# Splitting the end of a transformer block's backward pass into two streams with their own buffers

## The chip, the cores and the metric

The kernel runs on one core of one Trainium2 chip. The metric is the device time of one execution in microseconds, as the median of several runs. One further execution is taken with the hardware profiler; its page and its trace are what the text reads.

## The reference, cut to what matters

The program computes a decode step of a block (attention with a KV cache, then a ReLU MLP, each behind a layernorm) and all its gradients except for those of two constants. B = 2 sequences, D = 640, H = 32 heads of Dh = 128, Sk = 4096 cached positions, Dff = 1728, all in bfloat16.

```python
q = (x @ wq).reshape(B, Sq, Hq, Dh).transpose(0, 2, 1, 3)
scores = jnp.einsum("bhqd,bhkd->bhqk", q, k) * (Dh ** -0.5)
p = softmax(scores, axis=-1)
o = jnp.einsum("bhqk,bhkd->bhqd", p, v)
attn = o.transpose(0, 2, 1, 3).reshape(B, Sq, Hq * Dh) @ wo
...
h = x + A(layernorm(x), k_cache, v_cache, wq, wo)
h2 = h + relu(layernorm(h) @ w1) @ w2
_out, _vjp = jax.vjp(_f, A_x, A_k_cache, A_v_cache, A_wq, A_wo, B_w1, B_w2)
```

Outputs: out_0 is h2, out_1 the gradient of x, out_2 and out_3 those of the K and V caches (64 tiles of 1 MB each), out_4 that of wq (640 x 4096), out_5 of wo (4096 x 640), out_6 of w1 (640 x 1728), out_7 of w2 (1728 x 640). With one query position per sequence every gradient of a cache tile is an outer product of two vectors, and every gradient of a weight is a sum of two outer products, one for each sequence.

## The kernel before, in words

A *head* here is one of the 64 pairs of a sequence and a head. The work has two passes over the heads.

The first pass (`p1_iter`, 66 iterations, to about 500 us) loads K and V of each head, transposes K on TensorE, makes scores, softmax and the head's output. Between its steps run pieces of the small chains (`middle_gen`): the attention output, the MLP, the backward pass through it, and, head group by head group, the gradient that reaches each head's output (`go_group`). A chain may run ahead only as far as its results exist; the marks ("w1", b), ("gh1", b) and ("go", b, h) in `done` say how far it is.

The second pass (`p2_iter`, from iteration 44 of the first pass on beside it, from about 500 us on alone) loads V again for 53 of the heads (tile `Wt`; 11 are kept from the first pass). For a head j it transposes V in four groups of four fp32 transposes (L374), copies each from PSUM on ScalarE (`t_sb`, L379), multiplies them with the output's gradient (L387), and makes the two gradient tiles on VectorE: gV of head j from the softmax (L789, L791, the multiply is L735), and gK of head j - 1 (L769, L772), after `gsp` (L748), which needs the products of all four groups. Each half tile is one VectorE instruction. The stores of gK (L773) and gV (L792) are issued on GpSimd's queue (POOL); loads are issued on SyncE's (SP).

*Buffers.* 12 buffers of 8 KB per partition, each tagged by a home, serve everything of 1 MB: "ld" for loads and "g" for gradient tiles (3, then 4, then 5 of them). `take` hands out the one that came free first; `give` returns it in program order, so that whoever takes it next waits on the engine for its last use, also for a store that is still under way. The weight gradients' tiles `ot`, the pieces of wq that are read again (`wqs`) and the pieces of w2 read again (`w_t` in `mlp_out`) come out of "ld" as well, as long as one or two are free (`spare`, `reserve`).

*The end of the work.* When ("w1", 1) is done and the first pass is over, w1's memory is released and one background generator, `fin_gen`, is started in the queue `bg2`. In order it makes: rows of the MLP's activations (`rows_of`: a copy to `wide`, four matmuls with the identity, a copy back), out_7, rows, out_6, rows, out_5, in `outer_rows`. After each stored piece of out_6 and out_5 it may read one of six pieces of wq again (`gx_piece`: 30 transposes of wq, then 30 small matmuls into the x gradient), once all heads concerned have passed. Then come the rest of these pieces, the x gradient's layernorm backward, the two row stores of out_1, the rows of GQ and x1, and out_4. `outer_rows` makes three outer products of 512 or 128 columns into three PSUM banks ("mid", "m", "a"), casts them on ScalarE one after the other (L840), and stores a tile of about 1 MB from GpSimd's queue (L842). `store_row` (L572) transposes a row vector and stores it from SyncE's queue, out of one buffer `orow`.

*The order.* All instructions are placed by hand: the loop over `plan` steps `p2_iter`, and after each of its seven steps per head calls `bg_step`, which gives each background queue a credit (here `RATE2` = 0.85 per step); a generator yields what a piece of it costs (0.5 per outer product, 0.9 per eight wq transposes). Every engine executes its own instructions strictly in this order. What is left when the heads are through is run out at once (L1088 to L1091).

Of the kernel before, what the change touches and what calls it, by code (L numbers as in the profile page):

```python
# [15 lines left out]
def kernel(  # L16
# [60 lines left out]
    homes = {"ld": list(range(NBIG)), "g": []}  # L77
    free = {"ld": NBIG, "g": 0}
    owned = {"ld": NBIG, "g": 0}
    stores = [0]  # L80
    spare = [2]
    home_of = {}

    def take(tag, shape, name):
        assert free[tag] > 0, (tag, name)
        free[tag] -= 1
        k = homes[tag].pop(0)
        t = big.tile(shape, BF16, tag=f"big{k}", bufs=1, name=name)
        home_of[id(t)] = (tag, k, t)
        return t  # L90

    def give(t, to=None):
        tag, k, _ = home_of.pop(id(t))
        to = to or tag
        owned[tag] -= 1
        owned[to] += 1
        free[to] += 1
        homes[to].append(k)

    def share(n):  # L100

        stores[0] = n
        while owned["g"] < n and free["ld"] > 0:
            homes["g"].append(homes["ld"].pop(0))
            for d in (free, owned):
                d["ld"] -= 1
                d["g"] += 1
# [464 lines left out]
    def store_row(col_bf, n, dst):  # L572

        t = pst([16, 128], BF16, "mid", "row_ps")
        nc.tensor.transpose(t[0:n, :], col_bf, ident_bf[:])
        r = small.tile([16, 128], BF16, tag="orow", bufs=1, name="orow")
        nc.vector.tensor_copy(out=r[0:n, :], in_=t[0:n, :])
        nc.sync.dma_start(out=dst, in_=r[0:n, :])
# [47 lines left out]
    def mlp_out():  # L626

        ml32 = small.tile([128, ND, B], FP32, tag="ml32", bufs=1, name="ml32")
        nc.vector.memset(ml32[:], 0.0)
        for k in range(NW2):  # L630
            while free["ld"] < spare[0]:
                yield
            t = load_w2(k, "ld")
            yield from wait(8)
            c1 = min(NF, (k + 1) * FP)
            m_ps = pst([128, ND, B], FP32, "mid", "mlp_ps")
            for c in range(ND):
                for cf in range(k * FP, c1):
                    kc = f_kc(cf)
                    nc.tensor.matmul(m_ps[:, c, :], lhsT=t[0:kc, cf - k * FP, c * 128:(c + 1) * 128],  # L640
                                     rhs=acol[0:kc, cf, :], start=(cf == k * FP), stop=(cf == c1 - 1))
            give(t)
            yield
            nc.vector.tensor_tensor(out=ml32[:], in0=m_ps[:], in1=ml32[:], op=ALU.add)
        ml_bf = small.tile([128, ND, B], BF16, tag="ml_bf", bufs=1, name="ml_bf")
        nc.vector.tensor_copy(out=ml_bf[:], in_=ml32[:])
        y_bf = small.tile([128, B, ND], BF16, tag="y_bf", bufs=1, name="y_bf")
        nc.vector.tensor_tensor(out=y_bf[:].rearrange("p b c -> p c b"), in0=h1c[:], in1=ml_bf[:], op=ALU.add)
        yield from wait(3)
        for b in range(B):  # L650
            store_row(y_bf[:, b, :], ND, out_0[b].rearrange("s (c p) -> (s c) p", p=128))
            yield
# [87 lines left out]
    def p2_iter(j, busy):  # L740
# [45 lines left out]
        give(c["W"], "g" if owned["g"] < stores[0] else "ld")  # L786
# [31 lines left out]
    def outer_rows(L, nrow, R, N, out_ap, cc, between=None):  # L818


        P = nrow // cc
        grp = max(1, min(cc, 4096 // N))
        out_v = out_ap.rearrange("(p c) n -> p c n", c=cc)
        for c0 in range(0, cc, grp):
            gn = min(grp, cc - c0)
            while free["ld"] < spare[0]:
                yield
            ot = take("ld", [128, grp, N], "ot")
            todo = [(k, n0, min(512, N - n0)) for k in range(gn) for n0 in range(0, N, 512)]
            for t0 in range(0, len(todo), 3):  # L830
                part = []
                for k, n0, nn in todo[t0:t0 + 3]:
                    q = 32 * (fw[0] % 4)
                    o_ps = pst([128, 512], FP32, ("mid", "m", "a")[len(part)], "o_ps")
                    nc.tensor.matmul(o_ps[0:P, 0:nn], lhsT=L[q:q + B, bass.ds(c0 + k, P, step=cc)],
                                     rhs=R[q:q + B, n0:n0 + nn], start=True, stop=True)
                    part.append((o_ps, k, n0, nn))
                    fw[0] += 1
                for o_ps, k, n0, nn in part:
                    nc.scalar.copy(out=ot[0:P, k, n0:n0 + nn], in_=o_ps[0:P, 0:nn])  # L840
                yield 0.5 * len(part)
            nc.gpsimd.dma_start(out=out_v[:, c0:c0 + gn, :], in_=ot[0:P, 0:gn, :])  # L842
            give(ot)
            if between is not None:
                yield from between()

    def fin_gen(fin):
        gx1 = fin.tile([128, ND, B], FP32, tag="gx1", name="gx1")
        nc.vector.memset(gx1[:], 0.0)
# [3 lines left out]
        yield from wait(4)  # L853
        gx_next = [0]

        def gx_piece(k):

            hn = min(QP, H - k * QP)
            while free["ld"] < spare[0]:
                yield  # L860
            t = take("ld", [128, ND, QP * 128], "wqs")
            nc.sync.dma_start(out=t[:, :, 0:hn * 128], in_=wq_r[:, :, k * QP * 128:(k * QP + hn) * 128])
            yield from wait(6)
# [3 lines left out]
            for t0 in range(0, len(todo) + GT, GT):  # L867
                part = todo[t0:t0 + GT]
                nxt = None
                if part:  # L870
                    t_ps = pst([128, GT, 128], BF16, "tps", "t_ps")
                    for x, (c, j) in enumerate(part):
                        nc.tensor.transpose(t_ps[:, x, :], t[:, c, j * 128:(j + 1) * 128], ident_bf[:])
                    t_sb = mats.tile([128, GT, 128], BF16, tag="XT", bufs=5, name="t_sb")
                    nc.scalar.copy(out=t_sb[:, 0:len(part), :], in_=t_ps[:, 0:len(part), :])
                    nxt = (t_sb, part)
                    if t0 + GT >= len(todo):
                        give(t)
                    yield 0.9
                if prev is not None:  # L880
                    if acc is None:
                        acc = pst([128, ND, B], FP32, "m", "gx_ps")
# [4 lines left out]
                    yield  # L887
                prev = nxt
            nc.vector.tensor_tensor(out=gx1[:], in0=gx1[:], in1=acc[:], op=ALU.add)

        def gx_ready():

            k = gx_next[0]
            if k < NQ and all(("go", B - 1, h) in done for h in range(k * QP, min(H, (k + 1) * QP))):
                gx_next[0] += 1
                yield from gx_piece(k)

        yield from rows_of(fin, acol, NF, "ar", "rF")
        yield from rows_of(fin, gc, ND, "gr", "rD")
        yield from outer_rows(FIN["ar"], Dff, FIN["gr"], D, out_7, Dff // 96)  # L900
        yield from rows_of(fin, ghfc, NF, "ghfr", "rF")
        yield from rows_of(fin, x2c, ND, "x2r", "rD")
        yield from outer_rows(FIN["x2r"], D, FIN["ghfr"], Dff, out_6, ND, gx_ready)
        while ("gh1", B - 1) not in done:
            yield
        yield from rows_of(fin, OFc, H, "OFr", "rH")
        yield from rows_of(fin, gh1c, ND, "gh1r", "rD")
        yield from outer_rows(FIN["OFr"], HD, FIN["gh1r"], D, out_5, HD // 128, gx_ready)
        while gx_next[0] < NQ:
            yield from gx_ready()  # L910
            yield
# [4 lines left out]
        for b in range(B):  # L916
            gxo = small.tile([128, ND], BF16, tag="gxo", bufs=2, name="gxo")
            nc.vector.tensor_copy(out=gxo[:], in_=gx_bf[:, :, b])
            store_row(gxo[:], ND, out_1[b].rearrange("s (c p) -> (s c) p", p=128))
            yield  # L920
        yield from rows_of(fin, GQc, H, "GQr", "rH")
        yield from rows_of(fin, x1c, ND, "x1r", "rD")
        yield from outer_rows(FIN["x1r"], D, FIN["GQr"], HD, out_4, ND)
# [3 lines left out]
    bg2 = []  # L927
    done = set()
    credit = [0.0, 0.0]
# [15 lines left out]
    def bg_step(k, rate):  # L945
        step[0] += k
        q = (bg, bg2)[k]
# [17 lines left out]
    RATE2 = 0.85  # L965
# [30 lines left out]
    reserve = [0]  # L996

    def pump():
        while queue:
# [3 lines left out]
            else:  # L1003
                tag = "ld"
                if free["ld"] <= reserve[0]:
# [12 lines left out]
    fin = None  # L1018
# [12 lines left out]
    for n, (i, j) in enumerate(plan):  # L1031
# [3 lines left out]
        if j == 0:  # L1035
            stores[0] = 3
        if i is None and plan[n - 1][0] is not None:
            share(4)
        if j == H + KEPT[1]:
            share(5)  # L1040
# [6 lines left out]
        reserve[0] = 2 if bg2 and j is not None and j >= H + 4 else 0  # L1047
        spare[0] = 1 if j is not None and j >= H + 2 else 2
        if i is None and ("w1", 1) in done and fin is None:
            wts.release()  # L1050
            fin = tc.alloc_tile_pool(name="fin", bufs=1)
            bg2.append(("fin", fin_gen(fin)))
        if i == 12:
# [3 lines left out]
        if i is None:  # L1057
            spread[0] = 2
            k = 0
            while g2 is not None:  # L1060
# [5 lines left out]
                bg_step(1, RATE2)  # L1066
            continue
        at = MIXED if j is not None else REST
        for k, _ in enumerate(p1_iter(i, i < H + 1, int(H + 1 < i < P2_AT))):
# [15 lines left out]
            bg_step(1, RATE2)  # L1085
# [4 lines left out]
    while bg2:  # L1090
        bg_one(bg2)  # L1091
# [32 lines left out]
```

## Time and profile before

| | |
|---|---|
| median of 3 runs | 1010.29 us (1006.11 to 1011.26) |
| profiled execution, its own time | 1006.34 us |
| its span | 1004.6 us |
| PE, PEld, DVE, ACT, POOL busy | 786.2, 693.8, 657.1, 587.3, 108.3 us |
| mean granted clock of PE | 0.794 |
| HBM read, written | 212.16 MB, 149.13 MB |
| first and last ot cast (L840) | 692.0 and 997.1 us |
| wqs loads issued (L862), six | 746.5 to 917.9 us |
| last store of gV, of gK issued | 944.9 us, 952.7 us |

A page of the profile gives, for each engine, the busy time, then the span cut into 40 equal slices, then the DMA queues (q1 is the hardware queue of SyncE's loads, q0 the software queue of GpSimd's stores), the chain of work that ended last, and groups of instructions by source line. A line such as

```profile
L840 ACT CAST ot<-o_ps 128x512 bf16<-128x512 f32 (+4 forms) x160 | 66.3, 492 | 23.9 <-DMA out_dram<-ot 15.1
L842 POOL DMA_DIRECT2D out_dram<-ot x17: 519/531/547, 708.4 to 998.1; - x17
```

reads: line 840 of the kernel, on ScalarE, casts `o_ps` to `ot`, 160 times in five shapes, 66.3 us busy, 492 ns each on average; the engine stood idle 23.9 us just before such an instruction, most of it, 15.1 us, for the store of an `ot` tile. The second line (from the answer for one tile) gives shortest, median and longest duration in ns of the instruction that issues a store, and the first and last start in us. The duration is that of the issue, not of the transfer.

### The profile page before, as it was taken

Reading aid. Unit: us, or ns where it says so; the run is one execution under the profiler, and the core shown is the slowest. Engines: PE = TensorE matmul, PEld = TensorE weight load, DVE = VectorE, ACT = ScalarE, POOL = GpSimd, SP = SyncE. Lnnn points to the kernel's source line nnn. Section 1 sums busy time; section 2 is a strip of 40 time slices with the busy share of each in tenths; the row PEclk is TensorE's granted clock in tenths of the full one; section 3 lists DMA queues with packets and bytes.
Section 4 is the critical chain, followed back from the end, with each engine's and each line's share of the span. In section 5 each row is a group of like instructions: output and inputs, shape, how many; then the busy total and the mean of one; then the engine's idle time right before and its main releaser. Section 6 shows DMA issues by size and latency. Waiting matters only on the chain.

```text
span 1004.6 us, 30245 instructions
## 1 busy us (share of the span) xinstructions
PE 786.2 (78%) x13169; PEld 693.8 (69%) x13173; DVE 657.1 (65%) x1289; ACT 587.3 (58%) x1261; POOL 108.3 (11%) x219
## 2 busy tenths in 40 slices
PE   5999999999899989999968646558485938865846
PEld 5988898999888888888867545446364727654611
DVE  3555776755486687878788897998683726653600
ACT  4666666667677767777644433335363718554747
POOL 0000000000000010000012121212121212211201
PEclk8899999999799999999995756777565658555555
DMA  9999999995587799999999999999799998999735
GB/s 351 417 400 394 350 380 412 380 373 185 197 297 279 276 346 381 422 421 421 389 365 420 424 370 425 420 425 419 298 385 399 403 407 322 421 424 417 314 123 209
DMA packets 63205, 363.25 MB, mean 362 GB/s; under 512 B 5696, under 2 KB 20928, under 8 KB 22880
## 3 DMA queue, kind: packets, MB, share of 16 engines
q1 hardware_dynamic: 42416, 212.18, 54.3%
q0 software_dynamic: 20656, 149.14, 35.8%
q8 instruction: 103, 1.69, 0.7%
q14 instruction: 30, 0.25, 0.1%
HBM read 212.16 MB, written 149.13 MB: 360 GB/s over the span
## 4 chain that ended last, share of the span: by engine, by line
PE 45%; DMA 25%; DVE 10%; issue 10%; ACT 8%; POOL 1%; SPq 0%; POOLq 0%; DVEq 0%; ACTq 0%
PE t_ps L353 10%; PE m_ps L408 10%; DMA wqs<-in_A_wq_dram 8%; PE t_ps L374 7%; DMA out_dram<-gV 6%; DMA Kt<-in_A_k_cache_dram 5%; DMA out_dram<-gK 4%; PE m_ps L423 4%; DVE gV L735 4%; ACT t_sb L358 4%; PE s_ps L364 4%; DVE gK L735 3%; PE dp_ps L387 2%; ACT t_sb L379 1%; PE t_ps L345 1%
## 5 line engine op out<-in xcount | busy, mean ns | idle before, releaser
L358 ACT COPY t_sb<-t_ps 128x1024 bf16<-128x1024 bf16 x223 | 219.6, 1015 | 51.5 <-PE t_ps L353 49.4
L379 ACT COPY t_sb<-t_ps 128x512 f32<-128x512 f32 x256 | 148.9, 589 | 110.9 <-PE t_ps L374 107.9
L408 PE MATMUL m_ps<-pk,Vt 128*128 128x129 bf16 x2048 | 200.3, 225 | 4.3 <-issue 4.3
L374 PE MATMUL t_ps<-ident_f,Wt 128*128 128x128 f32 x848 | 186.5, 368 | 3.8 <-DMA Wt<-in_A_v_cache_dram 2.6
L735 DVE TENSOR_TENSOR gK<-rb,gsp 128x2048 bf16<-128x2048 bf16 x128 | 152.1, 1227 | 32.2 <-DMA out_dram<-gV 18.5
L415 DVE TENSOR_TENSOR pk<-Kt,ep 128x2048 bf16<-128x2048 bf16 x128 | 156.0, 1219 | 24.5 <-ACT ep L465 24.5
L735 DVE TENSOR_TENSOR gV<-rb,pp 128x2048 bf16<-128x2048 bf16 x128 | 152.2, 1218 | 23.1 <-DMA out_dram<-gK 11.1
L353 PE MATMUL t_ps<-ident_bf,Kt 128*128 128x128 bf16 x2048 | 153.0, 224 | 5.8 <-issue 3.8
L374 PEld LDWEIGHTS t_ps<-ident_f,Wt 128*128 128x128 f32 x848 | 133.0, 190 | 17.6 <-issue 9.3
L408 PEld LDWEIGHTS <-Vt 128*128 128x128 bf16 x2048 | 132.5, 101 | 14.3 <-issue 9.1
L353 PEld LDWEIGHTS <-Kt 128*128 128x128 bf16 x2048 | 126.7, 100 | 9.7 <-issue 5.2
L387 PEld LDWEIGHTS <-t_sb 128*128 128x128 bf16 x2048 | 91.5, 105 | 50.3 <-ACT t_sb L379 40.0
L387 PE MATMUL dp_ps<-gom,t_sb 128*128 128x2 bf16 x2048 | 94.3, 167 | 23.5 <-ACT t_sb L379 22.5
L364 PE MATMUL s_ps<-qc,t_sb 128*128 128x1 bf16 x2048 | 89.0, 164 | 13.4 <-ACT t_sb L358 9.5
L364 PEld LDWEIGHTS <-t_sb 128*128 128x128 bf16 x2048 | 79.4, 97 | 18.3 <-ACT t_sb L358 13.4
L840 ACT CAST ot<-o_ps 128x512 bf16<-128x512 f32 (+4 forms) x160 | 66.3, 492 | 23.9 <-DMA out_dram<-ot 15.1
L792 POOL DMA_DIRECT2D out_dram<-gV x64 | 34.2, 534 | 391.5 <-DVE gV L735 279.8
L356 DVE COPY t_sb<-t_ps 128x1024 bf16<-128x1024 bf16 x33 | 22.8, 691 | 68.3 <-PE t_ps L353 68.3
L518 ACT ACTIVATE MT<-m_ps,rtot 128x128 bf16<-128x128 f32 x64 | 23.6, 369 | 69.0 <-PE m_ps L408 64.7
L423 PE MATMUL m_ps<-ep,Kt 128*128 128x1 bf16 x2048 | 60.7, 163 | 1.3 <-ACT OU L519 1.2
L773 POOL DMA_DIRECT2D out_dram<-gK x64 | 34.0, 531 | 255.1 <-DVE gK L735 217.9
L423 PEld LDWEIGHTS <-Kt 128*128 128x128 bf16 x2048 | 58.4, 96 | 1.6 <-issue 1.1
(186 smaller groups left out, 871.2 us busy)
## 6 DMA issues: line engine op xcount, KB each, us to landing
Kt<-in_A_k_cache_dram SPq DMA_DIRECT2D x64, 1024.0 KB, 10.6
Vt<-in_A_v_cache_dram SPq DMA_DIRECT2D x64, 1024.0 KB, 8.6
out_dram<-gV POOLq DMA_DIRECT2D x64, 1024.0 KB, 11.3
out_dram<-gK POOLq DMA_DIRECT2D x64, 1024.0 KB, 11.1
Wt<-in_A_v_cache_dram SPq DMA_DIRECT2D x53, 1024.0 KB, 10.9
wo_t<-in_A_wo_dram SPq DMA_DIRECT2D x4, 1280.0 KB, 11.3
out_dram<-ot POOLq DMA_DIRECT2D x5, 1024.0 KB, 4.1
wq_t<-in_A_wq_dram SPq DMA_DIRECT2D x5, 960.0 KB, 10.3
```

Source lines behind the costliest of these rows:

```text
L353: nc.tensor.transpose(t_ps[:, j, :], nat[:, g * GT + j, :], ident_bf[:])
L358: nc.scalar.copy(out=t_sb[:], in_=t_ps[:])
L364: nc.tensor.matmul(dst[:, sc:sc + 1], lhsT=t_sb[:, j, :], rhs=vec, start=True, stop=True)
L374: nc.tensor.transpose(t_ps[:, j, :], natf[:, 2 * cc:2 * cc + 2, :].rearrange("p c k -> p (c k)"), ident_f[:])
L379: nc.scalar.copy(out=t_sb[:], in_=t_ps[:])
L387: nc.tensor.matmul(dst[:, sc:sc + 2], lhsT=v[:, j, :, par], rhs=vecs[:, par, :], start=(par == 0), stop=(par == 1))
L408: nc.tensor.matmul(r["m"][:, 0:129], lhsT=r["V"][:, sc, :], rhs=r["pk"][sc // HALF][:, sc % HALF, 0:129], start=False, stop=(sc == NSC - 1))
L415: nc.vector.tensor_tensor(out=p["pk"][k][:, :, 0:128].rearrange("p s (a two) -> p s a two", two=2), in0=p["K"][:, sl, :].rearrange("p s (a ...
L423: nc.tensor.matmul(r["m"][:, 129:130], lhsT=r["K"][:, sc, :], rhs=r["ep"][:, sc, 0:1], start=(sc == 0), stop=False)
L735: nc.vector.tensor_tensor(out=pairs_view(dst[:, sl, :]), in0=row.rearrange("p (a two) -> p a two", two=2)[:, None, :, :].to_broadcast([128 ...
L792: nc.gpsimd.dma_start(out=natural(out_3, b, h), in_=gV[:])
L840: nc.scalar.copy(out=ot[0:P, k, n0:n0 + nn], in_=o_ps[0:P, 0:nn])
```

## The change

The weight gradients and the x gradient become two background generators.

- *Two streams.* `fin_gen` now makes only the weight gradients, in the order out_7, out_6, out_5, out_4, the last two in two halves of 16 heads each. `gx_gen` makes the x gradient through wq, in a third queue `bg3` with a credit of its own (`RATE3` = 0.45 per step; `RATE2` is 0.65), from the time that the gradients of all heads' outputs exist.
- *Buffers.* Two more homes: "f" for `ot` tiles, "q" for pieces of wq and of w2. One more buffer of 8 KB (`big2`, in the memory that w1 leaves) is the first of home "f". `share` now states how many each home is to have; a buffer that is given back goes to the home that lacks one. When 36 heads of the second pass have begun: ld 4, g 4, f 3, q 2; when both streams are through: ld 7, g 6. Until then "f" has its one buffer and "ld" eight.
- *Outer products* go one by one through one PSUM bank, matmul and cast in separate steps; when the gradients of all heads' outputs exist, every third cast is done by VectorE (`late`). The tile is stored from ScalarE's queue.
- The x gradient's sums move from PSUM bank "m" to "a"; the next piece of wq is fetched as soon as a buffer of "q" is free; `orow` has two buffers.

```diff
-    homes = {"ld": list(range(NBIG)), "g": []}
-    free = {"ld": NBIG, "g": 0}
-    owned = {"ld": NBIG, "g": 0}
-    stores = [0]
-    spare = [2]
+    homes = {"ld": list(range(NBIG)), "g": [], "f": [], "q": []}
+    free = {tag: len(v) for tag, v in homes.items()}
+    owned = dict(free)
+    wanted = {}
+    pools = [big] * NBIG
...
+    def goes_to(tag):
+
+        if owned[tag] > wanted.get(tag, NBIG):
+            for other in homes:
+                if owned[other] < wanted.get(other, 0):
+                    return other
+        return tag
...
-        to = to or tag
+        to = to or goes_to(tag)
...
+    def more_home(tag, pool):
+        homes[tag].append(len(pools))
+        pools.append(pool)
+        free[tag] += 1
+        owned[tag] += 1
...
-        r = small.tile([16, 128], BF16, tag="orow", bufs=1, name="orow")
+        r = small.tile([16, 128], BF16, tag="orow", bufs=2, name="orow")
...
-            while free["ld"] < spare[0]:
+            while free["q"] < 1:
                 yield
-            t = load_w2(k, "ld")
+            t = load_w2(k, "q")
...
-            ot = take("ld", [128, grp, N], "ot")
+            ot = take("f", [128, grp, N], "ot")
             todo = [(k, n0, min(512, N - n0)) for k in range(gn) for n0 in range(0, N, 512)]
-            for t0 in range(0, len(todo), 3):
-                part = []
-                for k, n0, nn in todo[t0:t0 + 3]:
-                    q = 32 * (fw[0] % 4)
-                    o_ps = pst([128, 512], FP32, ("mid", "m", "a")[len(part)], "o_ps")
...
-                for o_ps, k, n0, nn in part:
+            for x, (k, n0, nn) in enumerate(todo):
+                q = 32 * (fw[0] % 4)
+                fw[0] += 1
+                o_ps = pst([128, 512], FP32, "m", "o_ps")
+                nc.tensor.matmul(o_ps[0:P, 0:nn], lhsT=L[q:q + B, bass.ds(c0 + k, P, step=cc)],
+                                 rhs=R[q:q + B, n0:n0 + nn], start=True, stop=True)
+                yield 0.3
+                if late[0] and x % 3 == 0 and x < len(todo) - 1:
+                    nc.vector.tensor_copy(out=ot[0:P, k, n0:n0 + nn], in_=o_ps[0:P, 0:nn])
+                else:
                     nc.scalar.copy(out=ot[0:P, k, n0:n0 + nn], in_=o_ps[0:P, 0:nn])
-                yield 0.5 * len(part)
-            nc.gpsimd.dma_start(out=out_v[:, c0:c0 + gn, :], in_=ot[0:P, 0:gn, :])
+                yield 0.3
+            nc.scalar.dma_start(out=out_v[:, c0:c0 + gn, :], in_=ot[0:P, 0:gn, :])
             give(ot)
-            if between is not None:
-                yield from between()
...
+    def gx_gen(fin):
...
+        def fetch():
+            while len(tiles) < NQ and free["q"] > 0:
+                k = len(tiles)
+                hn = min(QP, H - k * QP)
+                t = take("q", [128, ND, QP * 128], "wqs")
+                nc.sync.dma_start(out=t[:, :, 0:hn * 128], in_=wq_r[:, :, k * QP * 128:(k * QP + hn) * 128])
+                tiles.append(t)
+
+        while not all(("go", B - 1, h) in done for h in range(H)):
+            yield 0.0
...
-            share(4)
-        if j == H + KEPT[1]:
-            share(5)
+            share(ld=KEPT[1] + 3, g=4)
+        if fin is not None and not bg2 and not bg3:
+            share(ld=7, g=6)
+        elif fin is not None and j >= H + KEPT[1] - 1:
+            share(ld=4, g=4, f=3, q=2)
...
-        reserve[0] = 2 if bg2 and j is not None and j >= H + 4 else 0
-        spare[0] = 1 if j is not None and j >= H + 2 else 2
...
+            big2 = tc.alloc_tile_pool(name="big2", bufs=1)
+            more_home("f", big2)
             bg2.append(("fin", fin_gen(fin)))
+            bg3.append(("gx", gx_gen(fin)))
+        late[0] = all(("go", B - 1, h) in done for h in range(H))
```

## The prediction

> **What bounds the kernel now.** I read the 40 slices of the page first, then the busy time by stretches from 500 us on (the first pass over the heads ends at about 500 us, and nothing that the diff touches runs before 588 us), then who waited for whom on the engines and on SyncE's queue between 700 and 950 us, and last the timeline of the tail. The columns of the first fence are the stretch, its length, busy us and number of instructions of PE, PEld, DVE, ACT and POOL, the granted clock, the DMA share and GB/s.
>
> ```profile
> 500.00:600.00 100.00, 67.28 (x888) 59.84 (x886) 82.72 (x143) 42.90 (x91) 19.57 (x39) 0.67 0.99 396
> 600.00:700.00 100.00, 64.00 (x779) 54.75 (x777) 86.48 (x145) 43.33 (x88) 19.19 (x39) 0.70 1.01 420
> 700.00:750.00 50.00, 29.25 (x281) 22.08 (x282) 36.43 (x65) 25.75 (x65) 10.12 (x21) 0.57 0.89 343
> 750.00:825.00 75.00, 49.42 (x595) 42.72 (x593) 38.30 (x46) 33.99 (x62) 14.72 (x27) 0.59 1.00 406
> 825.00:840.00 15.00, 10.44 (x144) 9.34 (x144) 8.05 (x11) 8.27 (x15) 2.02 (x4) 0.63 0.64 228
> 840.00:925.00 85.00, 58.07 (x644) 46.83 (x641) 48.60 (x51) 46.31 (x99) 15.35 (x32) 0.62 1.01 422
> 925.00:955.00 30.00, 26.91 (x233) 18.75 (x231) 18.25 (x24) 22.41 (x53) 6.15 (x14) 0.56 0.81 328
> 955.00:1005.00 50.00, 25.09 (x83) 7.67 (x81) 1.70 (x10) 27.78 (x64) 3.60 (x7) 0.50 0.39 162
> ```
>
> From 600 us the DMA engines are the bound wherever they are fed: share 1.01 at 420 to 422 GB/s. There are three places where they aren't: 700 to 750 us, 825 to 840 us, and everything after 925 us, above all the last 50 us at 162 GB/s.
>
> ```profile
> PEld L873 <- DMA wqs<-in_A_wq_dram: 44.8, 4, 16.8
> DVE orow L577 <- DMA out_dram<-orow: 18.6, 1, 18.6
> ACT ot L840 <- DMA out_dram<-ot: 15.1, 1, 15.1
> SPq L395 <- DMA out_dram<-ot: 120.9, 5, 40.0
> 952.72 0.53 POOL L773 DMA_DIRECT2D out_dram<-gK  x1 [7.28 <-DVE lb_prod L233]
> 981.28 0.53 POOL L842 DMA_DIRECT2D out_dram<-ot  x1 [24.44 <-ACT ot L840]
> 998.06 0.53 POOL L842 DMA_DIRECT2D out_dram<-ot  x1 [3.66 <-ACT ot L840]
> ```
>
> The first four lines (waits, 700 to 950 us: total, times, longest) name the holes: PE stood 44.8 us for wq pieces, VectorE once 18.6 us for a row buffer, ScalarE once 15.1 us for a weight store to leave its buffer, and SyncE's queue held the loads of V 120.9 us for such stores. The last three (timeline) are the tail: the last store of the second pass is issued at 952.7 us, then come the x gradient's layernorm, the row copies of GQ and the five stores of out_4, the last at 998.1 us. Nothing of the second pass is left to run beside them.
>
> **What the Trainium skill says.** "DMA: Bandwidth & Descriptors", "Issuing engines are not separate DMA queues": transfers started by the scalar, sync and gpsimd engines share 16 engines, and more issuers save only issue time. The trace agrees: two queues together stop at 422 GB/s. So moving stores to ScalarE's queue brings no bandwidth. Its "Queues, rings and completion order" says that an engine takes the rows in turn, packet by packet; here POOL's queue moves stores while SyncE's loads, but no run here shows a third queue. Its "Anatomy of one DMA — SWDGE (gpsimd) path" says that a wait happens on the issuing sequencer, and prices a transfer at 2.0 us + bytes/436e3: 4.4 us for 1 MB. The trace has 4.1 us as the median of the 1 MB stores in the empty tail. "TensorE: Matmul & The Clock Gate", "Part 1: The HAM clock gate", says that a busy PE gets its full clock back; the trace has 0.70 at 64% busy and 0.50 in the tail, so denser PE work should not run slower.
>
> **The change part by part.** The sum is made on the profiled execution (span 1004.6, time 1006.34; the median of the runs is 1010.29).
>
> (1) *The floor.* Bytes from 600 us on, rate times length from the stretches: 42.0 + 17.2 + 30.5 + 3.4 + 35.9 + 9.8 + 8.1 = 146.9 MB. The change moves no byte away: same loads of V, wq and w2, same outputs. At 420 GB/s they take 350 us, so the span can't end before 950.
>
> (2) *The tail moves under the second pass.* In the order of the built program the outer products now start at head 22 (before: 33), the last weight store is issued at head 53, the x gradient's row leaves at head 55; after the last head nothing follows. The 50 us after 955 us go, and what they did (25.1 us of PE, 27.8 us of ScalarE) lies beside heads. What covers it: PE is busy 263.2 us of 405 from 600 us on; in a 375 us stretch that is 70%. VectorE: 238 us, and 23 casts that the change gives it, bounded by 0.35 and 0.7 us each (a 1024-column bf16 copy from PSUM took 691 ns): 16 us at most, in all 68%. If that cover were gone, PE or VectorE would set the pace; that is nearest between heads 41 and 53, where wq, w2 and out_4 come together: 13 heads of 4.8 us (64.0 us over the 13.3 heads of 600 to 700 us), 19 for the wq transposes, 7 for their products, 15 for 48 outer products, 8 for the rest, 111 us of PE beside 133 us of DMA (27.3 MB of gK and gV, 14.7 of V, 5.2 of wq, 2.2 of w2, 6.3 of weight gradients), 83%.
>
> (3) *Heads 57 to 63 only store.* All loads are issued by head 56. A head then is 2.1 MB, 5.2 us at the 403 GB/s that stores alone reach (371 GB/s at share 0.92 between 925 and 950 us), while VectorE needs 4 x 1.22 + 0.28 = 5.2 and PE's four groups about 5.2. I take 5.6 us, so 7 x (5.6 - 2.1/0.42) = 4 us over the floor, plus 4 us from the last issue to the last landing at less than the full rate: 8 us.
>
> (4) *Stores on ScalarE's queue.* 18 issues there. SyncE's wqs issue took 0.38 to 0.57 us, POOL's 0.53: at most 10 us of an engine that is under half busy, so nothing. Removing 17 issues from POOL frees nothing that anyone waited for. The cost is elsewhere: until head 36 the outer products have ONE buffer, and the order shows the next cast into it right behind its store on ScalarE after the stores of heads 24, 26, 30 and 31. ScalarE then stands until its own store has landed; behind it stand the t_sb copies of L379, hence PE's matvecs and VectorE's gsp and gK. Landing: 4.1 us (empty tail) to 19.6 us (slowest ot store); I take 8, since a store no longer queues behind gK and gV in POOL's queue and shares with one or two others. The cover is the stores already issued: four gradient buffers, 4.2 MB, 10 us. After the wait the pipeline needs four transposes of 1.2 us to the next gK. So 8 + 5 - 10 = 3 to 4 us of empty DMA each, bounded by 0 and by the 15.1 us of the case at 701 to 716 us. 4 x 3.5 = 14 us.
>
> (5) *Buffers of their own.* V loads no longer take turns with ot buffers, so the 120.9 us of SyncE's queue go, and bursts of five V loads ahead of a wq piece with them. From head 36 V has 4 buffers; four heads of some 9 us cover the 14.5 us that a load of V took there. Next late: wq pieces. There are two buffers, one of them shared with w2, and the order issues pieces 1 to 3 only 0.3 to 0.7 of a head before PE meets them. A piece of 0.96 MB behind one V or w2 load lands in 10 to 15 us: I expect PE to stand some 5 to 8 us a piece, 30 us against 44.8. That stretch (750 to 825 us) still moved 406 GB/s, so I price it at 0 to 15, value 6 us. The second row buffer removes the 18.6 us of VectorE; it is part of reaching the floor's rate.
>
> (6) *Serial casts.* Each outer product now waits for the cast before it (one PSUM bank instead of three), but one step of the loop lies between; 160 products of 0.31 us. Nothing taken, 0 to 10 us.
>
> Sum: 950 + 8 + 14 + 6 = 978, with the 1.7 us outside the span 980. The median stands 4 us above the profiled execution; one or two of these would fit here too, but I leave the number at 980.
>
> **The rivals.** *A, the sum:* 980, 60%. *B, the waits are hidden:* ScalarE's and PE's waits cost nothing, the DMA engines stay at 420: 978 - 20 + 2 = 960. For it: 600 to 700 us ran at 420 with PE at 64%. Against it: the hole at 712 us followed just such a ScalarE wait. 20%. *C, the tail is only traded:* heads 41 to 53 become PE's and cost twice their wait, 30 us instead of 6, and the casts their 10: 980 + 24 + 10 = 1014, no difference, about 8%. *D, slower:* the one buffer of heads 22 to 36. If each of its four waits costs a whole landing of 15 us and more, because the stores already issued have drained by then, the sum is 966 + 4 x 15.1 = 1026. It decides from (1015.3 - 966)/4 = 12.3 us each; against it stands the cover of 4.2 MB, and that ScalarE had only 43 us of work in 100 there. 12%. That the streams don't move is no rival: the order shows that they do.
>
> **How the numbers follow.** A measurement of this kernel can tell about 0.5% from no change, 1005.2 to 1015.3. Faster 0.80 (A, B), same 0.08 (C), slower 0.12 (D). The range leaves out D, C and the better end of B: 957, which is (1) to (3) without (4) to (6) less 3 us, to 1006, which is A with its costs at their upper ends in part.
>
> **What would show it.** Right: DMA share near 1.0 from 600 to about 930 us, no weight store after the last gK, ScalarE waiting four times for out_dram<-ot before 720 us, at some 8 us. Step 4 is wrong if those waits are over 12 us and the slices beside them fall under 350 GB/s; step 5 if PE waits over 60 us for wqs; step 2 if PE's or VectorE's busy share comes over 90% in a stretch while the DMA share falls.

## The result, and the profile after

| | before | changed |
|---|---|---|
| median | 1008.21 us (4 runs, 1006.11 to 1011.26) | 1070.38 us (4 runs, 1058.79 to 1076.63) |
| ratio, 95% interval | | 1.053 (1.045 to 1.061) |
| profiled execution, its span | 1006.34, 1004.6 us | 1076.13, 1074.4 us |

The change makes the kernel 5% slower; the forecast was 980 us, in a range of 957 to 1006. Two of the changed kernel's four executions were slow throughout, the profiled one among them, and so were the profiled ones of e5 and e8 below, so the ratios are made from the other executions alone. Some 16 us of the changed kernel's profiled execution lie ahead of head 21, in work that the change doesn't touch: its trace has the store of head 21's gV at 609.7 us, where that of e4, the same kernel but for one queue, has it at 593.3, like the kernel before. So the traces are compared from that store on.

| us, from the stores of gV in the trace | before | changed |
|---|---|---|
| head 21 to 41 | 156.2 | 223.0 |
| head 41 to 57 | 140.6 | 193.1 |
| head 57 to 63 | 54.8 | 37.4 |
| head 63 to the end | 59.7 | 11.2 |

The tail has gone as intended: 48 us less after head 63 and 17 between 57 and 63. But 119 us came in before that. The busy times by stretches of the changed kernel, columns as in the prediction's first fence:

```profile
600.00:650.00 50.00, 30.03 (x254) 23.50 (x254) 34.25 (x62) 21.81 (x52) 8.01 (x17) 0.57 0.92 359
650.00:700.00 50.00, 33.08 (x277) 26.61 (x277) 29.77 (x49) 22.39 (x52) 5.22 (x12) 0.50 0.70 253
700.00:750.00 50.00, 22.19 (x157) 13.26 (x156) 20.81 (x34) 16.78 (x35) 3.92 (x9) 0.53 0.68 261
950.00:1000.00 50.00, 33.59 (x317) 23.35 (x317) 23.94 (x38) 23.58 (x45) 3.92 (x9) 0.60 0.78 292
1000.00:1050.00 50.00, 39.03 (x461) 33.52 (x459) 34.06 (x39) 25.22 (x47) 10.59 (x21) 0.71 1.00 406
```

Where the kernel before kept the DMA engines at 420 GB/s, from 600 to 700 us, they now fall to 253, and in the next two lines to 261 and 292. No engine is busy in their place: in these three lines PE has 22 to 34 us of 50, VectorE 21 to 30, ScalarE 17 to 24. All of them have idle time at once, so they wait for each other in turn. Who waited for whom, from 590 us on (total in us, times, longest); the last line is SyncE's queue:

```profile
DVE gsp L765 <- PE dp_ps L404: 108.5, 23, 17.3
PE o_ps L853 <- ACT ot L859: 86.8, 90, 10.3
ACT ot L859 <- DMA out_dram<-ot: 29.9, 4, 10.3
PEld L923 <- DMA wqs<-in_A_wq_dram: 22.6, 3, 13.7
SPq L412 <- PE t_ps L391: 205.7, 18, 53.5
```

Three causes end in the first line: PE waits for ScalarE's casts (90 times), ScalarE for its own stores (4 times, and PE's 86.8 us hold these waits a second time, since PE stands behind ScalarE), PE for pieces of wq (3 times); VectorE then waits for PE before it can make gK. In the last line the loads of V wait until PE has done with a buffer: before, SyncE's queue waited for weight stores; now the DMA engines wait for PE.

Both kinds of ScalarE wait can be seen in the timeline of the changed kernel. First an ordinary stretch (start, length, what, and in brackets the idle time before it and what ended it):

```profile
656.28 1.11 PE L391 MATMUL t_ps<-ident_f,Wt 128*128 128x128 f32 x4
657.49 0.59 ACT L396 COPY t_sb<-t_ps 128x512 f32<-128x512 f32 x1 [1.45 <-PE t_ps L391]
657.97 0.26 ACT L859 CAST ot<-o_ps 96x128 bf16<-96x128 f32 x1
658.28 0.58 PE L853 MATMUL o_ps<-gr,ar 2*96 2x512 bf16 x1 [0.70 <-ACT ot L859]
658.79 1.11 PE L391 MATMUL t_ps<-ident_f,Wt 128*128 128x128 f32 x4
```

PE transposes a group; ScalarE can copy it only then, and only after that copy it casts the outer product that came before; PE's next outer product waits for that cast, since it needs the same PSUM bank, and the next transposes stand behind it. From one group of transposes to the next it is 2.51 us, with one product in between; with two products it is 3.3 us (650.49 to 653.82 in the same timeline). The kernel before, at the same granted clock of 0.50 and with the same 1.11 us for the transposes, has room for three products, in three banks, in 1.93 us:

```profile
695.60 1.11 PE L374 MATMUL t_ps<-ident_f,Wt 128*128 128x128 f32 x4
697.53 1.11 PE L374 MATMUL t_ps<-ident_f,Wt 128*128 128x128 f32 x4
```

A step without any product takes the same in both, 1.14 us (942.97 to 944.11 in the kernel before) and 1.16 us (683.55 to 684.71 in the changed one). Four groups make a head. Then a stretch with a store:

```profile
715.45 0.37 ACTq L861 DMA_DIRECT2D out_dram<-ot  x1
715.47 0.58 PE L853 MATMUL o_ps<-ghfr,x2r 2*128 2x512 bf16 x1 [0.76 <-ACT ot L859]
724.12 0.58 ACT L859 CAST ot<-o_ps 128x512 bf16<-128x512 f32 x1 [8.70 <-DMA out_dram<-ot]
724.75 0.58 PE L853 MATMUL o_ps<-ghfr,x2r 2*128 2x512 bf16 x1 [8.70 <-ACT ot L859]
726.93 0.28 DVE L765 SCALAR_TENSOR_TENSOR gsp<-dp_ps,negdot,P_bf 128x64 bf16<-128x64 f32 x1 [14.85 <-PE dp_ps L404]
```

ScalarE stands 8.7 us for the store that it has just issued, PE as long for ScalarE, VectorE 14.9 us for PE. That is the wait of the prediction's step 4. The four such waits are 4.8 to 10.3 us long, 7.5 in the mean, close to the 8 of the forecast; what they cost is not.

### The profile page after: what moved, and what is told of

Same layout as the page of the kernel before. It is cut to its first block, busy times and chain, and to the rows that moved or that the text cites. A ratio compares the mean times of both kernels' runs of the same rounds, so it can differ in the third digit from the quotient of the medians.

```text
span 1074.4 us, 30168 instructions
## 1 busy us (share of the span) xinstructions
PE 830.3 (77%) x13169; PEld 723.1 (67%) x13173; DVE 672.0 (63%) x1312; ACT 582.0 (54%) x1238; POOL 95.3 (9%) x202
## 4 chain that ended last, share of the span: by engine, by line
PE 55%; DMA 18%; ACT 13%; DVE 8%; issue 4%; POOL 0%; SPq 0%; ACTq 0%; POOLq 0%; DVEq 0%
PE t_ps L370 11%; PE t_ps L391 11%; PE m_ps L425 10%; DMA out_dram<-gV 7%; PE o_ps L853 6%; PE m_ps L440 4%; ACT t_sb L375 4%; PE s_ps L381 4%; DMA wqs<-in_A_wq_dram 4%; ACT ot L859 3%; DVE gV L752 3%; DMA out_dram<-ot 3%; ACT t_sb L396 3%; DMA Kt<-in_A_k_cache_dram 2%; PE dp_ps L404 2%
## 5 line engine op out<-in xcount | busy, mean ns | idle before, releaser
L425 PE MATMUL m_ps<-pk,Vt 128*128 128x129 bf16 x2048 | 205.1, 229 | 4.5 <-issue 4.4
L391 PE MATMUL t_ps<-ident_f,Wt 128*128 128x128 f32 x848 | 190.0, 372 | 1.4 <-DMA Wt<-in_A_v_cache_dram 1.3
L370 PE MATMUL t_ps<-ident_bf,Kt 128*128 128x128 bf16 x2048 | 161.9, 232 | 6.0 <-DMA Kt<-in_A_k_cache_dram 3.5
L752 DVE TENSOR_TENSOR gK<-rb,gsp 128x2048 bf16<-128x2048 bf16 x128 | 152.3, 1225 | 20.0 <-DMA out_dram<-gK 12.3
L425 PEld LDWEIGHTS <-Vt 128*128 128x128 bf16 x2048 | 136.2, 103 | 14.5 <-issue 9.1
L370 PEld LDWEIGHTS <-Kt 128*128 128x128 bf16 x2048 | 134.6, 104 | 9.9 <-DMA Kt<-in_A_k_cache_dram 3.7
L404 PEld LDWEIGHTS <-t_sb 128*128 128x128 bf16 x2048 | 94.5, 106 | 57.8 <-ACT t_sb L396 27.2
L381 PE MATMUL s_ps<-qc,t_sb 128*128 128x1 bf16 x2048 | 89.9, 164 | 13.7 <-ACT t_sb L375 8.6
L381 PEld LDWEIGHTS <-t_sb 128*128 128x128 bf16 x2048 | 81.1, 98 | 19.0 <-ACT t_sb L375 12.7
L765 DVE SCALAR_TENSOR_TENSOR gsp<-dp_ps,negdot,P_bf 128x64 bf16<-128x64 f32 x64 | 18.0, 281 | 112.8 <-PE dp_ps L404 112.6
```

What stands on the lines that cost most here:

```text
L370: nc.tensor.transpose(t_ps[:, j, :], nat[:, g * GT + j, :], ident_bf[:])
L381: nc.tensor.matmul(dst[:, sc:sc + 1], lhsT=t_sb[:, j, :], rhs=vec, start=True, stop=True)
L391: nc.tensor.transpose(t_ps[:, j, :], natf[:, 2 * cc:2 * cc + 2, :].rearrange("p c k -> p (c k)"), ident_f[:])
L404: nc.tensor.matmul(dst[:, sc:sc + 2], lhsT=v[:, j, :, par], rhs=vecs[:, par, :], start=(par == 0), stop=(par == 1))
L425: nc.tensor.matmul(r["m"][:, 0:129], lhsT=r["V"][:, sc, :], rhs=r["pk"][sc // HALF][:, sc % HALF, 0:129], start=False, stop=(sc == NSC - 1))
L752: nc.vector.tensor_tensor(out=pairs_view(dst[:, sl, :]), in0=row.rearrange("p (a two) -> p a two", two=2)[:, None, :, :].to_broadcast([128 ...
```

## The experiments

Theories: **W**, ScalarE's wait for its own store (one buffer); **B**, PE's wait for the cast before (one PSUM bank); **L**, wq pieces fetched too late; **Q**, ScalarE's queue itself. Each kernel was timed beside the kernel before, and a ratio is its time over that one's. A gain in us below is a difference of two ratios times 1008 us; the intervals of the ratios leave each gain uncertain by some 10 us.

**e1, the wait.** Half the tile, so two buffers in the same memory:

```diff
-        grp = max(1, min(cc, 4096 // N))
+        grp = max(1, min(cc, 2048 // N))
...
             more_home("f", big2)
+            more_home("f", big2)
...
-            share(ld=4, g=4, f=3, q=2)
+            share(ld=4, g=4, f=4, q=2)
```

> The changed kernel with the weight gradients stored in tiles of half the size, so that the memory of the one buffer of home f holds two of them (f=4 instead of 3 later): a cast on ScalarE no longer waits for the store issued just before it, but for the one before that. Theory W (ScalarE's waits for its own store, with all that is queued behind them, cost what heads 24 to 33 lost, about 57 us by the trace): the waits ACT ot <- DMA out_dram<-ot fall from 29.9 us to under 8, heads 24 to 33 lose under 20 us, the time falls by 35 to 50 us to 1015 to 1030. Theory B (one PSUM bank makes PE wait for each cast; 86.8 us of PE waits for ACT ot in the trace): the time falls by 15 us at most.

Measured: 1032.03 us, ratio 1.018 (1.009 to 1.027), against 1.053: 35 us. Its waits:

```profile
ACT ot L859 <- DMA out_dram<-ot: 2.9, 1, 2.9
PE o_ps L853 <- ACT ot L859: 64.0, 93, 1.6
```

W holds, at about 35 us. The edit also halves the tile, which was not run apart; but the waits for stores are gone (2.9 us of 29.9 are left), as two buffers would have it. Heads 21 to 41 still take 198.1 us, and the waits for casts are as many as in the changed kernel (93, now none over 1.6 us): B is another cost.

**e2, the bank.** Two PSUM banks in turn:

```diff
-                o_ps = pst([128, 512], FP32, "m", "o_ps")
+                o_ps = pst([128, 512], FP32, ("m", "mid" if late[0] else "a")[x % 2], "o_ps")
```

> The changed kernel with the outer products put alternately into two PSUM banks (m and a; m and mid once the x gradient's stream runs) instead of one. Theory B: PE's waits for ACT ot fall from 86.8 us to under 45 and the time falls by 30 to 50 us. Theory W: the four waits of 5 to 10 us and their heads stay as they are, PE merely meets the next copy behind the same standing ScalarE; the time falls by 10 us at most.

Measured: 1027.08 us, ratio 1.015 (1.009 to 1.022): 38 us.

```profile
PE o_ps L853 <- ACT ot L859: 40.0, 27, 11.1
ACT ot L859 <- DMA out_dram<-ot: 37.1, 4, 11.1
PEld L923 <- DMA wqs<-in_A_wq_dram: 36.9, 5, 13.0
```

B holds too. The casts that PE waits for fall from 90 to 27, and what is left (longest 11.1 us) is for the most part the four store waits, which stay. Neither theory's "at most 10 or 15 us for the other" was right: both are there. PE, now earlier, waits longer for wq, 36.9 us instead of 22.6.

**e3, both.** The two edits together.

> Half tiles and two banks together. If W and B are both part of it and independent, the gain is the sum of the two single ones. If what is left is the wq pieces and the crowding of heads 42 to 53, the time stays over 1000; if W and B are all of it, it comes to 975 to 990, as the sum in the prediction has it without them.

Measured: 1001.91 us, ratio 0.994 (0.990 to 0.998), a gain of 59 us. The single gains sum to 35 + 38 = 73; so the two are in the main separate costs, and the intervals don't tell whether they overlap by the rest. Heads 21 to 41 now take 172.0 us, but heads 41 to 57 take 186.7, little less than in the changed kernel (193.1): the third cost is there, and untouched.

```profile
PEld L923 <- DMA wqs<-in_A_wq_dram: 39.0, 5, 11.6
PE o_ps L853 <- ACT ot L859: 20.9, 27, 5.0
```

**e4, the queue.** `nc.gpsimd.dma_start` instead of `nc.scalar.dma_start` for the weight stores, nothing else.

> The changed kernel with the weight stores issued from GpSimd's queue again, all else as it is. Theory W: the buffer is still one, so ScalarE still waits for the landing of its last store, now from behind gK and gV in one queue: landing 10 to 15 us instead of 5.7, the waits grow from 29.9 to 40 to 60 us, the time grows by 10 to 30 us. Theory Q (the queue on ScalarE itself is the harm: issue and lane waits in ScalarE's order): the time falls by 15 us or more.

Measured: 1060.02 us, ratio 1.049 (1.040 to 1.057): not told from the changed kernel's.

```profile
ACT ot L859 <- DMA out_dram<-ot: 30.7, 4, 10.5
```

ScalarE still waits four times, and the stores land in 6.6 us (median; 5.7 from ScalarE's queue). So Q falls, and so does what I expected of W: a store behind gK and gV in one queue was not late. Perhaps little is queued ahead of it where the DMA share is only 0.68 to 0.82, as it is from 600 to 750 us in e4; that was not tested.

**e5, the pieces of wq.** On e3, `share(ld=4, g=4, f=3, q=3)` instead of `f=4, q=2`.

> The kernel of e3 (half tiles, two banks) with three buffers in home q and three in f (instead of two and four): wq pieces 1 to 3 are then fetched about two heads before PE meets them, though w2 holds one buffer. In e3 PE waits 39.0 us for wq pieces and heads 41 to 57 take 187 us, against 136 us before (head 41 to 57) and 164 us reckoned from the bytes. Theory L (late pieces): PE's waits for wqs fall under 12 us, heads 41 to 57 take 160 to 167 us, the time falls by 20 to 27 us to 975 to 982. Theory C (crowding: PE, ScalarE and VectorE in one fixed order with too much between the heads' own steps): the waits move to others (t_sb copies, casts), heads 41 to 57 stay over 180 us, the time falls by 7 us at most.

Measured: 980.13 us, ratio 0.970 (0.965 to 0.975), 24 us below e3. The waits of its trace:

```profile
DVE gsp L765 <- PE dp_ps L404: 35.8, 18, 5.9
PE o_ps L853 <- ACT ot L859: 24.8, 27, 4.2
PEld L923 <- DMA wqs<-in_A_wq_dram: 11.7, 2, 10.2
```

PE's 39.0 us of waits for wq pieces in e3 fall to 11.7, heads 41 to 57 take 162.4 us (186.7 in e3): L holds, C falls. VectorE's wait for PE, the end of all three chains, is a third of the changed kernel's 108.5 us.

**e6, the casts on VectorE.** On e5, `if False:` in place of the condition with `late`.

> The kernel of e5 with all casts of the outer products on ScalarE (the late third on VectorE undone). In e3 VectorE waited 29.1 us for products that PE had not made yet, with gK and gV queued behind. Theory V (these waits hold up the gradient tiles): the time falls by 8 to 20 us against e5. Theory A (ScalarE is the scarcer of the two there, 23 casts of 0.6 us more): the time grows by 5 to 15 us. Neither: within 4 us.

Measured: 978.55 us, ratio 0.969 (0.963 to 0.974): no difference. Taking VectorE's 19.9 us of waits for products away and giving ScalarE the casts comes to nothing that can be measured; two opposite effects of the edit would not be told from none.

**e7, the queue once more, on e6.** The stores from GpSimd's queue.

> The kernel of e6 (half tiles, two banks, three buffers in q, casts on ScalarE) with the weight stores on GpSimd's queue again. In e6 the DMA share stands at 0.97 to 1.00 from 600 to 850 us, but at 379 to 387 GB/s where the kernel before moved 420 at the same share. If the third queue is what makes the packets slower, two queues move 405 or more there and the time falls by 8 to 15 us, under 971. If not (small tiles or the loads of 1536-byte rows do it), the time stays within 5 us, or grows by up to 8 us because a weight store then waits behind gK and gV.

Measured: 983.67 us, ratio 0.975 (0.970 to 0.980). The intervals of e6 and e7 overlap, and the two move about the same in the first stretch (of e6, then of e7): no sign that the third queue makes the packets slower.

```profile
600.00:650.00 50.00, 40.24 (x326) 29.63 (x325) 36.44 (x59) 28.08 (x67) 7.60 (x18) 0.57 1.00 385
```

```profile
600.00:650.00 50.00, 41.22 (x332) 29.44 (x330) 37.60 (x60) 28.46 (x69) 12.32 (x23) 0.57 0.98 380
```

**e8, the third buffer of q alone.** On the changed kernel, `share(ld=4, g=4, f=2, q=3)`.

> The changed kernel with three buffers in home q and two in f (instead of two and three), nothing else: the single part that e5 added to e3. If the wq pieces cost the same with the other two costs in place: PE's waits for wqs fall from 22 us to under 8 and the time falls by 12 to 22 us against the changed kernel. If the late pieces only decide once PE is no longer held up by casts: 8 us at most, since PE then comes later to each piece anyway; heads 24 to 33 lose their 57 us in either case.

Measured: 1042.89 us, ratio 1.030 (1.024 to 1.037): 23 us. Heads 41 to 57 take 168.8 us instead of 193.1, heads 21 to 41 are unchanged at 224.9. In its trace PE doesn't wait for a wq piece at all. So L costs about the same whether the other two are there (23 us) or not (24).

**e9, three banks,** on e6: `(("m", "mid") if late[0] else ("m", "a", "mid"))[x % (2 if late[0] else 3)]`.

> The kernel of e6 with three PSUM banks in turn for the outer products until the x gradient's stream begins (then two). In e6 PE still waits 24.2 us for casts. If these are the bank's: they fall under 12 us and the time by 4 to 10 us. If they are ScalarE standing for a store (12.8 us left) or the DMA engines are the bound by now: within 4 us.

Measured: 975.98 us, ratio 0.965 (0.958 to 0.972), the lowest median of all; its interval overlaps e6's, so the third bank's 4 us are not told from none. PE's waits for casts fall from 24.2 to 16.9 us, not under the 12 expected. Its tail is the new one:

```profile
900.00:950.00 50.00, 37.28 (x429) 32.19 (x429) 33.23 (x38) 22.66 (x43) 10.21 (x19) 0.64 1.01 418
964.19 0.53 POOL L790 DMA_DIRECT2D out_dram<-gK  x1 [2.06 <-DVE gK L752]
```

The DMA engines are full from 900 to 950 us, and the last store, a gK, is issued at 964.2 us of a span of 972.8.

**b1, two row buffers in the kernel before:** `bufs=2` for `orow`.

> The kernel before with two row buffers orow instead of one, the single part of the change that removes VectorE's 18.6 us wait at 813 to 831 us. If that wait made the hole at 825 to 840 us (228 GB/s), 15 us at 190 GB/s under the full rate are 7 us of DMA time: the time falls by 4 to 8 us. If the wait for the wq piece at 816 to 829 us makes the hole anyway: 0 to 3 us.

Measured: 998.28 us, ratio 0.987 (0.982 to 0.993), a gain of some 13 us, more than the 4 to 8 expected. The hole of the kernel before at 825 to 840 us (228 GB/s) is filled:

```profile
825.00:840.00 15.00, 12.53 (x150) 11.40 (x150) 7.27 (x9) 8.19 (x14) 1.76 (x4) 0.50 1.01 414
```

**b2, ScalarE's queue in the kernel before:** `nc.scalar.dma_start` for the weight stores.

> The kernel before with the weight stores issued from ScalarE's queue, the single part of the change that e4 undid. From e4 (within its interval of the changed kernel) and from 17 issues of some 0.35 us: no difference, within 5 us. If ScalarE's issue waits for the landing of earlier transfers that share a semaphore with it, ScalarE stands and the time grows by over 8 us.

Measured: 997.79 us, ratio 0.989 (0.982 to 0.996): a small gain, which I did not expect. In its trace ScalarE waits 7.8 us for a weight store instead of 15.1, and from 700 to 750 us 379 GB/s are moved instead of 343. That this is why was not tested. The prediction's "frees nothing that anyone waited for" does not hold for the kernel before.

**b3, b1 and b2 together.**

> The kernel before with both single parts: two row buffers and the weight stores on ScalarE's queue. b1 alone gave a ratio of 0.987, b2 alone 0.989. If they mend different places (the hole at 825 to 840 us there, the waits for weight stores at 700 to 750 us and the last stores here), the ratio is 0.974 to 0.980, about 984 to 988 us. If both mend the same hole: 0.985 to 0.990.

Measured: 996.45 us, ratio 0.990 (0.987 to 0.993, 20 runs). They don't add up: together they are worth what each is worth alone. Which wait takes the place of the one removed is open.

## Why the prediction was wrong, step by step

**Right: the bytes of step 1, the move of step 2, the tail of step 3, and the list of waits.** No weight store follows the last gK; heads 57 to 63 and what comes after take 37.4 + 11.2 us, where step 3 comes to 7 x 5.6 + 4 = 43. ScalarE waits exactly four times for its own store, 7.5 us each where I said 8; PE waits for wq pieces 22.6 us where I said 30. The waits were named and measured off rightly. Their *price* was too low, in each of three steps. (One statement on the change is wrong: `share(ld=7, g=6)` moves no buffer when both streams are through. A buffer leaves only a home that holds more than `wanted` has for it, and "f" and "q" have no entry there; the homes stay at ld 4, g 4, f 3, q 2. Nothing here shows that it costs time.)

**Step 6, wrong, the largest.** "Nothing taken, 0 to 10 us", because one step of the loop lies between cast and next product. The bank costs 38 us by itself (e2) and 24 us once the buffer is mended (e1 to e3). A step of the loop is an order, not a time: ScalarE's cast stands behind a copy that can't begin before PE's transposes end, so PE's transposes, copy, cast and product run one after the other: 2.51 us for a group with one product, where the kernel before had a group with three in 1.93; a group with two takes 3.3 us in the changed kernel and 2.1 with two banks (e2, 660.08 to 662.16 us of its timeline). I had the duration of the product alone (0.31 us) where the round trip counts.

**Step 4, mis-sized: 14 us, measured 35 (e1).** That is some 9 us for each wait, where I had 3 to 4: a wait of 8 and a refill of 5, less 10 for the stores already issued. The stretch beside the wait shown above, and the one behind it (columns as above):

```profile
715.50:724.00 8.50, 0.55 (x1) 0.09 (x1) 0.00 (x0) 0.00 (x0) 0.00 (x0) 0.50 0.81 290
724.00:732.00 8.00, 5.96 (x35) 3.40 (x35) 4.93 (x10) 4.64 (x9) 0.53 (x1) 0.50 0.14 58
```

While ScalarE stands, the DMA engines still have work for 0.81 of the time. They run dry behind the wait: no gradient tile has been made meanwhile, and loads of V wait for PE. The empty DMA time is 0.19 x 8.5 + 0.86 x 8 = 8.5 us, an estimate from these two lines, and as much as a wait cost. So the cover was some 8 us and not 10, and the refill took 8 us and not 5. My sign for a wrong step 4 (waits over 12 us, and slices beside them under 350 GB/s) asked for longer waits than it takes. With the two banks already in place the buffer costs 22 us (e2 to e3), which the intervals don't tell from 35. The point from which rival D decides, 12.3 us each, was not reached; whether the buffer alone would have made the kernel slower was not run.

**Step 5, mis-sized: 6 us, measured 23 (e8) and 24 (e3 to e5).** I priced PE's waits by the 406 GB/s that the DMA engines moved in a stretch with such waits in the kernel before. During the longest wait of the changed kernel (13.7 us) they move 369, and again run dry behind it:

```profile
943.00:957.00 14.00, 0.33 (x6) 0.27 (x4) 1.43 (x2) 0.61 (x2) 0.77 (x2) 0.50 0.92 369
957.00:966.00 9.00, 8.06 (x120) 7.43 (x117) 4.20 (x5) 7.62 (x15) 0.53 (x1) 0.78 0.39 132
```

**The sum.** The single gains are 35 + 38 + 23 = 96 us, all three together 84 (1.053 to 0.970). So the three account for all of the slowdown, and what is left of the change is worth 3%. That e5 takes 980.13 us, the number that I gave for the changed kernel, is luck: without the waits of steps 4 and 5, which e5 has for the most part mended, my sum has 960. By estimate the rest lies in the rate: the floor of step 1 is made on 420 GB/s, and e6, which takes as long as e5, moves 383 in the mean from 600 to 850 us, which is worth 22 us. The rivals were built one mechanism each. C did have the crowding, but gave it 34 us in all; D had the direction, but only the buffer; none had three moderate costs on one chain, which is what happened.

**The range** failed for the same reason: its upper end took step 6 at 10 us at most. The page of before could have bounded it from above: its 160 casts are 66.3 us, and with one bank PE may have to stand through each.

**The clock, wrong, but not a cause.** From 0.70 at 64% busy I concluded that denser PE work should not run slower. The line of e6 above has PE 80% busy, at a granted clock of 0.57. It isn't what slows the changed kernel: that has the same 0.57 from 600 to 650 us, and in e6 the loss is gone.

**Open:** why the mended kernels move only 375 to 394 GB/s from 600 to 700 us at a DMA share near 1.0, where the kernel before moved 420. Neither the third queue (e7) nor the half tiles, with their rows of 3456 and 3840 bytes, are needed for it: the changed kernel, with whole tiles, moves 359 GB/s at a share of 0.92 from 600 to 650 us, and e4, with whole tiles and two queues, 312 at 0.82, which is 390 and 380 at a share of 1.

## What to carry to other kernels

A wait is free only while something else is behind; read that from the stretch as the change will leave it, not as it is, and look at what runs dry behind the wait as well as beside it. When side work is woven into an in-order pipeline, give each staging step two buffers, in PSUM and in SBUF alike, before it is started early: a step's round trip through two engines counts, not its busy time. Fetch side data a full step of the main work ahead of its use, with a buffer that nothing else takes.

## What the runs showed of the hardware that I had not expected

- A store issued from ScalarE's queue occupied its sequencer for 0.32 to 0.39 us (18 issues) and landed in 2.6 to 15.6 us, 5.7 us in the median, while two other queues were in use; from GpSimd's queue (e4) the same stores landed in 6.6 us.
- Stores alone came close to the rate of mixed traffic: in e6, after all loads, 410 GB/s from 950 to 967 us, against 420 in the kernel before from 600 to 700 us. The gradient tiles follow each other at 5.0 to 5.2 us a head of 2.1 MB there, and VectorE is busy for 16.5 of these 17 us, so the stores alone may reach more.
- PE's granted clock in the changed kernel was 0.92 from 100 to 450 us, at 93% busy, and 0.50 to 0.60 from 600 to 1000 us, at 44 to 73% busy. "TensorE: Matmul & The Clock Gate", "Part 1: The HAM clock gate", has a busy PE get its full clock back; over stretches of 50 us the busy share alone does not show that, since e6 has 0.50 to 0.57 at 80 to 88% busy from 600 to 750 us.
